# One condition in a list scheduler's port model: small two-input VectorE operations and GpSimd

## The chip, the cores and the metric

The kernel runs on one core of a Trainium2 chip. The metric is the device time of one execution in microseconds, the median of several runs. A profiled execution has a time of its own, which is given beside the length of its trace, the span.

## The reference: what is computed

The input x has 2048 tokens of 512 elements. It is normalised per token, and the result is the sum of x, a linear attention block on the normalised tokens and a dense block on the same.

```python
xn = _layernorm(x)                       # 2048 x 512, eps 1e-5
q, k, v = split(xn @ wqkv)               # 32 heads of 16
phi = lambda t: where(t > 0, t + 1, exp(t)) + 1e-6
kv = sum over tokens of phi(k) v^T       # per head
z  = sum over tokens of phi(k)
o  = (phi(q) kv) / (phi(q) z + 1e-6)
A  = o @ wo
B  = relu(xn @ w1 + b1)**2 @ w2 + b2     # 1376 hidden
out = x + A + B
```

Everything is float32. The kernel splits each operand of a product into a high and a low part in a faster TensorE format and adds three products, so each logical matmul is three of 128x512.

## The kernel before, in words

The token axis is cut into 16 tiles of 128 (NT), grouped in 4 blocks of 512 (NB, TB = 4).

**First part: keys.** For each tile i the kernel takes mean and variance on VectorE (measure: bn_stats, bn_aggr), the root on ScalarE (roots: Ln, then Exp), three small VectorE operations that refine it and the scaling itself (normalise). The scaled tile xp[i] is turned, by TensorE for the first 8 tiles (turned_pe) and by DMAs with a VectorE transpose for the others, and split in high and low (transposed: tiles xs0h, xs0l, xs1h, xs1l). TensorE then forms the key projection (project, tiles pk in PSUM), ScalarE and VectorE apply phi and split the result (phi_k, parts: tiles k and pk), ScalarE and GpSimd split the scaled tile itself (tokens: tile tok, the only large work of GpSimd), and TensorE accumulates xp^T phi(k) over all tiles (kx).

**Second part.** The queries, the attention's output and the dense block are done for two pairs of blocks with one level of Strassen's scheme: weights and their sums are split into operands (ops) that go out to DRAM (wd) and come back, the tokens' sums (T) likewise stay on chip, hidden values (rr, rf, c) are squared or divided, split on ScalarE and VectorE (parts_of: tiles s), and multiplied into PSUM (second).

**The order of the work is planned, not written.** The function body doesn't issue instructions. `nc` is a Program whose engines are Recorders; each call becomes a Task with its predecessors (add), and a duration from a formula (cost). emit then asks order for a sequence and issues it. order plays the list up to 150 times (ROUNDS):

- play is a list scheduler with one lane per engine. TensorE's tasks, and all tasks recorded ahead of `nc.fixed = len(nc.tasks)` (set after kx(0)), keep their recorded order on their engine. Behind that, each of VectorE, ScalarE, GpSimd and SyncE picks, among the tasks that are ready within 0.1 us, the one with the earliest due time.
- press looks at every wait of TensorE over 0.1 us in that play, follows the chain of causes back and moves the due times of the tasks on it earlier.
- The play with the earliest end gives the order that is issued.

Two engines meet in the model at one more point. A task with `lock` set starts no earlier than the end of the last locked task, and holds the lock for its own length:

```python
            if t.lock:
                t.start = max(t.start, locked)
                locked = t.start + t.dur
```

GpSimd's tensor_tensor has the lock (in this kernel the low halves of tok, and one of wkl). VectorE's tensor_tensor and scalar_tensor_tensor have it when no input is in PSUM and, before the change, when the output has more than 64 elements per partition. In cost, n is that number of output elements, and src the largest count of any operand. VectorE's two-input operations are modelled at 0.157 us + src/960.

The operations with two inputs in SBUF and 64 elements or fewer are the three refining ones of normalise, on 1 to 3 elements (one per tile of the group):

```python
        nc.vector.scalar_tensor_tensor(u, var, 1e-5, y0, op0=OP.add, op1=OP.mult)
        nc.vector.scalar_tensor_tensor(u, u, -0.5, y0, op0=OP.mult, op1=OP.mult)
        nc.vector.scalar_tensor_tensor(r, u, 1.5, y0, op0=OP.add, op1=OP.mult)
```

They write tile y. The groups of tiles are (0), (1), (2), (3), (4, 8, 9), (5, 10), (6, 11), (7, 12), (13, 14) and (15); normalise of the first four is recorded ahead of nc.fixed, of the others behind it. Since every instruction is issued from emit, nearly all lines of the profile carry its line, L301, and groups are told apart by their tiles.

Of the kernel before, what the change touches and what calls it, by code (L numbers as in the profile page):

```python
# [74 lines left out]
class Program:  # L75
# [59 lines left out]
    def cost(self, t, out, ins):  # L135
        n = 1
        for s, k in list(out.ap)[1:]:
            n *= k
        src = n
        for a in ins:  # L140
            m = 1
            for _, k in list(a.ap)[1:]:
                m *= k
            src = max(src, m)
        t.lock, t.size, t.lag = False, 0, 0.06
        if t.engine == "tensor":
            wide = t.name == "matmul" and ins[0].dtype != F32
            t.dur, t.lag = (0.0135 + n / 2400 if wide else 0.055 + n / 2400 if t.name == "transpose" else 0.11 + n / 1200), 0.23
        elif t.engine == "scalar" and t.name != "dma_start":
            ps = any(map(in_psum, ins))  # L150
            t.dur = (0.2 if ps else 0.22) + src / 1250 + (0.09 if t.kw.get("bias") is not None and n > 64 and not isinstance(t.kw.get("bias"), float) else 0)
        elif t.engine == "vector":
            a, b = self.DVE.get(t.name, (0.1, 0.5))
            t.dur = a + src * b / 960
            t.lock = t.name in ("tensor_tensor", "scalar_tensor_tensor") and n > 64 and not any(map(in_psum, ins))
        elif t.engine == "gpsimd" and t.name != "dma_start":
            t.dur = 0.2 + src * 2.3 / 1000 if t.name == "tensor_tensor" else 0.3
            t.lock = t.name == "tensor_tensor"
        else:
            b = 1  # L160
            for s, k in out.ap:
                b *= k
            run = 1
            for a in (out, *ins):
                d = list(a.ap)
                c = d[-1][1] if d[-1][0] == 1 else 1
                run = min(run, c) if run > 1 else c
            t.size, t.lag = 4 * b, 2.8 if b > P * P else 2.0
            t.dur = 0.43 if out.ap[0][1] == P and run >= 512 else 0.62 if ins and isinstance(ins[0], View) and isinstance(out, View) else 0.5 if t.engine != "gpsimd" else 1.2
            t.size = t.size * max(1.0, (0.009 + run * 4 / 27e3) / (run * 4 / 24e3)) if run > 1 else b * 150  # L170
# [1453 lines left out]
```

## Time and profile before

| what | value |
|---|---|
| time, median of 3 runs | 409.05 us (408.73 to 409.63) |
| time of the profiled execution | 408.82 us |
| its span | 407.1 us |
| TensorE busy | 399.6 us in 1793 matmuls and transposes |
| VectorE busy | 353.2 us in 600 instructions |
| ScalarE busy | 269.4 us in 461 instructions |
| GpSimd busy | 28.0 us in 50 instructions |
| DMA | 95.68 MB, mean 235 GB/s |
| granted TensorE clock | 0.999 |

PE is TensorE, PEld its weight loads, DVE VectorE, ACT ScalarE, POOL GpSimd, SP SyncE. A row of a group gives its engine and operation, output<-inputs by tile name (buffer numbers left out), shapes, count, then busy time, mean duration in ns, and the idle time of the engine just before, with what ended it. A row of the chain or of the order of time begins with start and length in us. A row by stage gives the stage, its length, and the busy time and count of each engine.

### The profile page before, as it was taken

What the parts mean: (1) busy time and instruction counts of PE and PEld (TensorE: products, weight loads), DVE (VectorE), ACT (ScalarE), POOL (GpSimd) and SP (SyncE); (2) the same over time, 40 slices, a digit from 0 to 9 for tenths busy, and PEclk for the clock granted to TensorE, in tenths of its full rate; (3) what the DMA queues carried; (4) which work ended last, traced back from release to release, by engine and by line L of the source; (5) the groups of instructions that cost most, each with busy time, mean ns of one, the idle gap of its engine ahead of it and who ended that gap; (6) DMA issues with size and microseconds to landing.
All of it is one profiled execution on the core that took longest, in us unless ns stands there. A gap on an engine that the chain in (4) does not pass through costs nothing.

```text
span 407.1 us, 5594 instructions
## 1 busy us (share of the span) xinstructions
PE 399.6 (98%) x1793; PEld 330.4 (81%) x1793; DVE 353.2 (87%) x600; ACT 269.4 (66%) x461; POOL 28.0 (7%) x50
## 2 busy tenths in 40 slices
PE   8999999999999999999999999999999999999994
PEld 7787888788888888888888888888888888888883
DVE  5899898799878898999889989899989989786784
ACT  5785665675858897889886343366888777545440
POOL 2232322220000000000000000000000000000001
PEclk9999999999999999999999999999999999999999
DMA  7871455933997679667359998999767789979424
GB/s 230 292 194 43 104 155 125 280 100 151 327 323 287 233 280 306 248 241 260 155 194 361 258 339 275 370 298 330 280 223 271 263 219 258 256 277 281 157 54 103
DMA packets 78674, 95.68 MB, mean 235 GB/s; under 512 B 39186, under 2 KB 50450, under 8 KB 78388
## 3 DMA queue, kind: packets, MB, share of 16 engines
q1 hardware_dynamic: 76404, 94.53, 73.4%
q10 hardware_dynamic: 2144, 0.52, 0.6%
q0 software_dynamic: 96, 0.26, 0.3%
q8 instruction: 14, 0.23, 0.2%
q14 instruction: 16, 0.13, 0.1%
HBM read 57.81 MB, written 35.39 MB: 229 GB/s over the span
## 4 chain that ended last, share of the span: by engine, by line
PE 95%; DVE 2%; DMA 1%; ACT 1%; issue 0%
PE ps L301 52%; PE acc L301 42%; DMA x<-in_A_x_dram 1%; DVE y L301 1%; DVE xp L301 0%; DVE res L301 0%; DVE o L301 0%; DVE st L301 0%; ACT k L301 0%; DVE pk L301 0%; DVE xs0l L301 0%; ACT t L301 0%; ACT xs0h L301 0%; DVE mv L301 0%
## 5 line engine op out<-in xcount | busy, mean ns | idle before, releaser
L301 PE MATMUL ps<-s,ops 128*128 128x512 f32 x405 | 94.9, 389 | 0.0
L301 PEld LDWEIGHTS ps<-s,ops 128*128 128x128 f32 x405 | 76.0, 188 | 15.8
L301 PE MATMUL acc<-s,ops 128*128 128x512 f32 (+1 forms) x270 | 62.2, 382 | 0.0
L301 PEld LDWEIGHTS acc<-s,ops 128*128 128x128 f32 x270 | 49.6, 188 | 9.9
L301 ACT ACTIVATE s<-rr 128x512 fp32r<-128x512 f32 x54 | 33.8, 631 | 20.9 <-DVE s L301 12.0
L301 PE MATMUL acc<-pk,tok 128*128 128x512 f32 x192 | 47.2, 394 | 0.0
L301 DVE TENSOR_TENSOR s<-rr,s 128x512 fp32r<-128x512 f32 x54 | 36.8, 688 | 11.8 <-ACT s L301 10.6
L301 PEld LDWEIGHTS acc<-pk,tok 128*128 128x128 f32 x192 | 35.4, 188 | 8.3 <-DVE pk L301 0.6
L301 PE MATMUL ps<-T,ops 128*128 128x512 f32 x168 | 41.4, 390 | 0.0
L301 PE MATMUL acc<-T,ops 128*128 128x512 f32 x168 | 41.2, 389 | 0.0
L301 PEld LDWEIGHTS acc<-T,ops 128*128 128x128 f32 x168 | 31.5, 188 | 6.6
L301 PEld LDWEIGHTS ps<-T,ops 128*128 128x128 f32 x168 | 31.5, 188 | 6.5
L301 POOL TENSOR_TENSOR tok<-xp,tok 128x512 fp32r<-128x512 f32 x16 | 21.5, 1347 | 43.8 <-ACT tok L301 43.8
L301 PE MATMUL ps<-xs0h,ops 128*128 128x512 f32 x72 | 23.7, 389 | 0.0
L301 ACT ACTIVATE rr<-acc 128x512 f32<-128x512 f32 x23 | 13.6, 589 | 11.5 <-PE acc L301 11.1
L301 DVE TENSOR_TENSOR ops<-raw,ops 128x512 fp32r<-128x512 f32 (+1 forms) x28 | 18.7, 676 | 1.6 <-ACT ops L301 1.6
L301 ACT ACTIVATE ops<-raw 128x512 fp32r<-128x512 f32 (+1 forms) x28 | 15.8, 576 | 5.2 <-PE acc L301 1.8
L301 PE MATMUL acc<-xs0h,ops 128*128 128x512 f32 x56 | 18.4, 389 | 0.0
L301 DVE TENSOR_TENSOR rr<-acc,rr 128x512 f32<-128x512 f32 x21 | 14.4, 687 | 2.9 <-PE acc L301 1.6
L301 POOL DMA_DIRECT2D out_dram<-res x2 | 1.5, 729 | 215.5 <-DVE res L301 213.0
L301 ACT ACTIVATE k<-ps 128x512 f32<-128x512 f32 x16 | 9.5, 593 | 10.1 <-PE ps L301 9.9
L301 PEld LDWEIGHTS ps<-xs0h,ops 128*128 128x128 f32 x72 | 13.5, 188 | 2.8
(158 smaller groups left out, 772.1 us busy)
## 6 DMA issues: line engine op xcount, KB each, us to landing
wd<-ops SPq DMA_DIRECT2D x35, 512.0 KB, 4.8
ops<-wd SPq DMA_DIRECT2D x31, 512.0 KB, 5.5
ops<-wd SPq DMA_DIRECT2D x56, 256.0 KB, 4.1
wd<-made SPq DMA_DIRECT2D x10, 512.0 KB, 5.9
res<-in_A_x_dram SPq DMA_DIRECT2D x32, 128.0 KB, 5.6
wd<-ops SPq DMA_DIRECT2D x13, 256.0 KB, 3.7
out_dram<-res SPq DMA_DIRECT2D x24, 128.0 KB, 4.7
x<-in_A_x_dram SPq DMA_DIRECT2D x5, 512.0 KB, 5.9
```

The source lines that it names most:

```text
L301: getattr(getattr(self.nc, t.engine), t.name)(*map(real, t.args), **{k: real(a) for k, a in t.kw.items()})
```

## The change

One line of cost loses one condition, so that VectorE's tensor_tensor and scalar_tensor_tensor have the lock at any size when no input is in PSUM. Durations, predecessors, first due times and the recorded list of tasks stay; so do all instructions and their operands. What can differ is the order in which VectorE, ScalarE, GpSimd and SyncE issue theirs.

```diff
         elif t.engine == "vector":
             a, b = self.DVE.get(t.name, (0.1, 0.5))
             t.dur = a + src * b / 960
-            t.lock = t.name in ("tensor_tensor", "scalar_tensor_tensor") and n > 64 and not any(map(in_psum, ins))
+            t.lock = t.name in ("tensor_tensor", "scalar_tensor_tensor") and not any(map(in_psum, ins))
```

## The prediction

> **What bounds the kernel now.** I read the page from the top: span, busy time by engine, granted clock by slices.
>
> ```profile
> span 407.1 us, 5594 instructions
> PE 399.6 (98%) x1793; PEld 330.4 (81%) x1793; DVE 353.2 (87%) x600; ACT 269.4 (66%) x461; POOL 28.0 (7%) x50
> PEclk9999999999999999999999999999999999999999
> ```
>
> TensorE is busy for 98% of the span at the full granted clock, and VectorE for 87%. The two lie that close, so the question is where TensorE ever waits. The table by stage tells it:
>
> ```profile
> 23.30:48.00 24.70, 24.24 (x114) 19.58 (x113) 23.56 (x52) 16.70 (x36) 7.21 (x10) 1.00 0.37 92
> 48.00:90.00 42.00, 41.99 (x186) 34.46 (x185) 36.49 (x55) 27.06 (x50) 11.69 (x17) 1.00 0.62 166
> 90.00:150.00 60.00, 60.00 (x283) 50.24 (x282) 52.14 (x88) 45.65 (x77) 0.00 (x0) 1.00 0.76 267
> 150.00:250.00 100.00, 100.00 (x443) 82.81 (x442) 91.75 (x149) 71.59 (x118) 0.52 (x1) 1.00 0.79 262
> 250.00:350.00 100.00, 100.00 (x443) 82.77 (x442) 91.88 (x155) 69.67 (x115) 0.00 (x0) 1.00 0.89 273
> 350.00:399.00 49.00, 49.00 (x218) 40.58 (x217) 36.65 (x56) 22.65 (x37) 0.80 (x1) 1.00 0.66 199
> ```
>
> After the length of a stage come the busy times of TensorE, its weight loads, VectorE, ScalarE and GpSimd. Between 48 and 399 us TensorE is busy for 350.99 of 351 us. In 23.3 to 48 it idles for 0.46 us, and there VectorE is busy for 23.56 of 24.70 us (95%): this is the stage in which VectorE is the one that is late. What is left of the span is the start and the tail after the last matmul.
>
> The list of TensorE's own waits names the place, and the chain that ended last shows the same stretch in order of time:
>
> ```profile
> PE ps L301 <- DVE xp L301: 0.5, 1, 0.5
> ```
>
> ```profile
> 17.14 2.89 PE acc L301 x12
> ...
> 20.47 3.01 PE acc L301 x12
> ...
> 30.40 1.18 DVE y L301
> ...
> 33.25 2.76 PE acc L301 x12
> 36.01 3.30 PE ps L301 x16
> 39.30 2.77 PE acc L301 x12
> 42.07 3.16 PE ps L301 x16
> 45.23 2.77 PE acc L301 x12
> 48.01 2.72 PE ps L301 x12
> ...
> 77.93 3.01 PE acc L301 x12
> 80.94 2.72 PE ps L301 x12
> ```
>
> Twelve matmuls take 2.72 us when nothing holds them (the rows at 48.01 and 80.94). From the excess of the other rows I count what TensorE loses to late operands: 0.17 + 0.29 at 17 and 20 us, 0.46 before the row at 33.25, 0.04 + 0.05 + 0.05 in the rows of 2.76 and 2.77, 0.14 in 3.30 against 3.16, and 0.29 at 77.93. That is **1.5 us in the whole kernel**, the most that a better order of the same work can win between start and tail.
>
> **The change part by part.** No instruction is added, removed or resized. The lock flag of the planner's VectorE two-input tasks loses its condition n > 64. The only tasks with two on-chip inputs and at most 64 elements are the three scalar_tensor_tensor of each normalise (tile y, 1 to 3 elements): ten groups, 30 tasks. Four groups lie ahead of nc.fixed, where every engine keeps its recorded order, and six behind it, 18 tasks. In the planner's play these 18 now start only when GpSimd's last tensor_tensor is done. Do they wait on the chip? The rows of groups and of time say yes:
>
> ```profile
> L301 POOL TENSOR_TENSOR tok<-xp,tok 128x512 fp32r<-128x512 f32 x16 | 21.5, 1347 | 43.8 <-ACT tok L301 43.8
> L301 DVE SCALAR_TENSOR_TENSOR y<-mv,y 128x2 f32<-128x2 f32 x4 | 3.6, 908 | 0.1
> L301 DVE SCALAR_TENSOR_TENSOR y<-mv,y 128x1 f32<-128x1 f32 x5 | 0.7, 147 | 0.0
> ```
>
> ```profile
> 30.02 1.53 POOL L301 TENSOR_TENSOR tok<-xp,tok 128x512 fp32r<-128x512 f32 x1 [3.21 <-ACT tok L301]
> ...
> 30.32 1.25 DVE L301 SCALAR_TENSOR_TENSOR y<-mv,y 128x2 f32<-128x2 f32 x1
> ...
> 31.99 1.92 DVE L301 TENSOR_SCALAR xp<-x,mv,y 128x512 f32<-128x512 f32 x4
> ...
> 32.59 0.65 PE L301 MATMUL ps<-ident,xp 128*128 128x128 f32 x4 [0.46 <-DVE xp L301]
> ```
>
> A two-element operation has a mean of 908 ns where its one-element sister has 147, and the one at 30.32 ends at 31.57, 0.02 us after GpSimd's at 31.55. The Trainium skill, SBUF — State Buffer, section "Who interferes with whom", says that a VectorE instruction with two SBUF inputs contends with a GpSimd instruction that reads SBUF; the trace agrees, down to two elements. By that rule alone the new model is the truer one and the sum would be the gain below without the loss.
>
> **The gain.** Four two-element operations cost 4 x (0.908 - 0.147) = 3.0 us of VectorE time that the present plan doesn't know of. They are on the end's path only where TensorE waits: behind the operation at 30.32 stand the other two y operations, the scaling to xp and then TensorE's transposes, which start 0.46 us late. With the 0.14 of the row at 36.01 I put the aimed gain at **0.6 us**. Its bounds are 0 (the planner finds no better place in a stage where VectorE is 95% busy) and 1.5 us (all excess goes).
>
> **The loss.** The plan is the best of 150 rounds of a greedy play; each round moves due times by the waits of the round before, and an operation is chosen among those ready within 0.1 us. A start that shifts by 1 us at 30 us changes these choices all the way down. So VectorE, ScalarE, GpSimd and SyncE get another order between 23 and 399 us, not only around y, while TensorE keeps its own. Behind 48 us the present order loses 0.3 us. The new one can't win there, and it has these margins:
>
> ```profile
> L301 ACT ACTIVATE s<-rr 128x512 fp32r<-128x512 f32 x54 | 33.8, 631 | 20.9 <-DVE s L301 12.0
> L301 DVE TENSOR_TENSOR s<-rr,s 128x512 fp32r<-128x512 f32 x54 | 36.8, 688 | 11.8 <-ACT s L301 10.6
> DVE s L301 <- ACT s L301: 15.6, 27, 1.0
> ```
>
> VectorE has 8.2 us free in each 100 us of the two long stages, and much of its idling is already the second half of a split waiting for ScalarE's first half (27 times, 15.6 us). Where another order lets a split slip by one place, TensorE waits for one VectorE operation (0.69) or the pair (0.63 + 0.69 = 1.32 us). What a new order costs is not in the trace. From below it is 0 (the model's orders hold on the chip as this one does); from above I take four whole splits, 4 x 1.32 = 5.3 us. The nearest row is a slip of one VectorE operation, 0.69 us, and I take three in 351 us: **2.1 us**. That "three" is a choice, not a reading; the only firm support is that the present count is nearly zero and can only rise.
>
> Queues: the DMAs of xTd, wd and ops are SyncE tasks and move with the plan too. The queues gain nothing to issue, so I cost that at nothing; the cover is the DMA engines' share, 0.62 to 0.89 in the stages behind 48 us. If it is gone, a late ops tile costs up to the 5.5 us from issue to landing, which I leave outside the sum:
>
> ```profile
> ops<-wd SPq DMA_DIRECT2D x31, 512.0 KB, 5.5
> ```
>
> Sum against the profiled execution: 408.82 (span 407.1 and 1.7 around it) - 0.6 + 2.1 = 410.3. The median of the runs lies 0.23 above that execution, so **410.5 us**.
>
> **Rivals.**
> *Only the gain.* The search is good enough to leave TensorE unbroken behind 48 us again. For it: the modelled costs are plainly close (the present order holds for 351 us), and the change mends a wait that was modelled as nothing. Time: 409.05 - 0.6 = 408.45, and with all excess gone 407.55; as a case I centre it on 408.1. It decides from the point at which the row at 33.25 starts without the 0.46 and no new wait stands behind 48 us. Chance 0.32.
>
> *The wait changes its owner.* The planner puts the y operations ahead of GpSimd's tok, and the next VectorE operation of the group, the scaling to xp, meets it instead, unmodelled before and after:
>
> ```profile
> 55.34 1.34 POOL L301 TENSOR_TENSOR tok<-xp,tok 128x512 fp32r<-128x512 f32 x1 [3.74 <-ACT tok L301]
> 55.44 1.52 DVE L301 TENSOR_SCALAR xp<-x,mv,y 128x512 f32<-128x512 f32 x1
> L301 DVE TENSOR_SCALAR xp<-x,mv,y 128x512 f32<-128x512 f32 x16 | 9.2, 600 | 0.3
> ```
>
> The scaling at 55.44 takes 1.52 against a mean of 0.60, some 0.9 us of waiting. Paid once in place of the 1.1 of the y at 30.32, it gives 409.05 - 0.2 = 408.9. The Trainium skill (SBUF — State Buffer, the same section) lists tensor_scalar among the operations that can take the shared ports; the row above agrees, and by that rule the change mends half of the group. Chance 0.2, together with an order that hardly changes or whose gain and loss cancel, within 0.3 us of 409.05.
>
> *The change does nothing* would need that no y met a lock in the model; the four groups of two elements stand so near to tok that I count it in the chance above.
>
> **How the numbers follow.** Forecast (slower, 410.5) 0.48, only the gain 0.32, owner or cancelling 0.2. The forecast's own range is 409.7 to 413.7 (one slip without the gain, 0.69, to four whole splits less the gain: 409.05 + 5.3 - 0.6). The range of all takes in the other cases: low 407.5 (all excess gone), high 413.5. About 0.2% (0.8 us) is what a measurement of this kernel can tell from no change, since three runs span 408.73 to 409.63. Of the 0.32, 0.24 lies beyond that, the rest is the same; of the forecast 0.45 lies beyond. So faster 0.24, same 0.31 (0.2 + 0.08 + 0.03), slower 0.45.
>
> **What would show it.** The gain: two-element y operations at 0.15 to 0.2 us, TensorE without idle time in 23 to 48 us, VectorE's busy time in that stage down by up to 3 us. The loss: pieces of the chain behind 48 us longer than 2.72 per twelve matmuls, and ACT or VectorE s, ops, rr or T as releaser of TensorE in the list of waits. The owner's rival: xp operations over 1 us in greater number. The forecast is wrong if TensorE's busy time between 48 and 399 is whole again, or if the loss sits in the start or the tail, which I hold still: the last store ends on the same chain of transposes and adds whatever the plan.

## The result, and the profile after

| | before | after |
|---|---|---|
| median of the runs (the three of before above are among its six) | 409.35 us (408.73 to 410.06, 6 runs) | 407.72 us (407.62 to 408.01, 6 runs) |
| profiled execution, its span | 408.82, 407.1 us | 408.01, 406.3 us |

The ratio is 0.9961, 95% interval 0.9948 to 0.9974: **faster by 0.4%**, 1.6 us, where slower by 0.35% (410.5 us) was forecast. The time lies below the forecast's own range, 409.7 to 413.7, and inside the range of all cases, 407.5 to 413.5. The sign is the other one.

The table by stage of the changed kernel, and TensorE's list of waits:

```profile
23.30:48.00 24.70, 24.70 (x118) 20.42 (x117) 22.46 (x53) 17.48 (x38) 7.44 (x12) 1.00 0.46 114
48.00:90.00 42.00, 42.00 (x187) 34.79 (x186) 36.61 (x56) 26.15 (x47) 12.56 (x15) 1.00 0.58 168
90.00:150.00 60.00, 60.00 (x282) 50.24 (x282) 49.59 (x83) 46.87 (x79) 0.00 (x0) 1.00 0.75 259
150.00:250.00 100.00, 100.00 (x443) 82.81 (x442) 92.50 (x150) 70.20 (x115) 0.52 (x1) 1.00 0.81 251
250.00:350.00 100.00, 100.00 (x443) 82.75 (x442) 91.64 (x155) 71.38 (x116) 0.00 (x0) 1.00 0.94 289
350.00:399.00 49.00, 49.00 (x221) 40.66 (x220) 38.78 (x60) 22.18 (x36) 0.79 (x1) 1.00 0.66 193
```

```profile
PE ps L301 <- DVE odds L301: 1.1, 1, 1.1
PE acc L301 <- DVE y L301: 0.3, 1, 0.3
```

Between 23.3 and 48 us TensorE idled 0.46 us before; now 24.70 of 24.70 us are busy. Behind 48 us it is unbroken again. The two waits left stand in the first 8 us. The chain of the changed kernel:

```profile
20.68 2.99 PE acc L301 x12
23.67 3.17 PE ps L301 x16
26.84 2.75 PE acc L301 x12
29.60 3.16 PE ps L301 x16
32.76 2.77 PE acc L301 x12
35.53 3.16 PE ps L301 x16
38.69 2.75 PE acc L301 x12
...
77.30 2.72 PE acc L301 x12
80.02 2.72 PE ps L301 x12
```

From the row at 20.68 to that at 32.76 are 12.08 us; before it was 33.25 - 20.47 = 12.78. The y, xp and ACT steps that stood in this chain before are gone from it, and at 77.30 a plain 2.72 stands in place of 3.01. The rows of 2.99 and of 2.75 to 2.77 are nearly as long as before. The y operations themselves, by group and in order of time:

```profile
L301 DVE SCALAR_TENSOR_TENSOR y<-mv,y 128x2 f32<-128x2 f32 x4 | 0.6, 161 | 0.7 <-ACT y L301 0.7
L301 DVE SCALAR_TENSOR_TENSOR y<-y 128x1 f32<-128x1 f32 x10 | 3.1, 305 | 0.3
```

```profile
28.42 0.16 DVE L301 SCALAR_TENSOR_TENSOR y<-mv,y 128x2 f32<-128x2 f32 x1 [0.45 <-ACT y L301]
28.61 0.36 DVE L301 SCALAR_TENSOR_TENSOR y<-y 128x2 f32<-128x2 f32 x2
29.01 0.55 DVE L301 TENSOR_SCALAR xp<-x,mv,y 128x512 f32<-128x512 f32 x1
```

The group that ran at 30.3 us, just behind GpSimd's tok, now runs at 28.4, ahead of it, and the mean of the two-element operation falls from 908 to 161 ns. Two one-element ones behind 46 us wait now (1.02 us at 47.12, 0.76 at 54.17; the mean of the ten goes from 176 to 305 ns), where TensorE isn't held by them.

**A ledger.** TensorE does the same matmuls in the same order in every kernel of this study, so its time can be compared piece by piece. The columns, called periods below, run from the first weight load of kx for tile 2 to that for tile 3, from 3 to 4, 4 to 5, 10 to 13, and from there to the last weight load of the program, in us of the profiled execution. Tiles 5 to 10 are left out: they take the same time in every kernel but e2.

| kernel | 2-3 | 3-4 | 4-5 | 10-13 | 13-end |
|---|---|---|---|---|---|
| before | 6.60 | 6.05 | 5.93 | 16.61 | 312.49 |
| before, second profile (e4) | 6.61 | 6.05 | 5.93 | 17.28 | 312.45 |
| after | 5.92 | 5.93 | 5.91 | 16.32 | 312.50 |

Against the least seen (5.92, 5.92, 5.91, 16.32) the order before loses 0.7 + 0.1 us at tiles 2 to 4 in each profile, and 0.29 in one and 0.96 in the other at tiles 10 to 13. The changed kernel loses nothing. The sum, 1.1 to 1.8 us, has the measured 1.6 within it. The start of the program, up to the first of these loads of tile 0, is recorded ahead of nc.fixed and has the same order in all of them; it differs from execution to execution (16.6 to 17.1 us in these three), which is why the spans of the two first profiles differ by 0.8 only. The last column is the one to keep in mind: **312.5 us in all three**.

### The profile page after: what moved, and what is told of

Read it like the earlier page. It is cut to its first block, busy times and chain, and to the rows that moved or that the text cites. A ratio compares the mean times of both kernels' runs of the same rounds, so it can differ in the third digit from the quotient of the medians.

```text
span 406.3 us, 5591 instructions
## 1 busy us (share of the span) xinstructions
PE 399.2 (98%) x1793; PEld 330.8 (81%) x1793; DVE 351.6 (87%) x600; ACT 270.2 (66%) x461; POOL 28.9 (7%) x50
## 4 chain that ended last, share of the span: by engine, by line
PE 96%; DVE 1%; DMA 1%; issue 0%
PE ps L301 53%; PE acc L301 43%; DMA x<-in_A_x_dram 1%; DVE res L301 0%; DVE o L301 0%; DVE st L301 0%; DVE xp L301 0%; DVE y L301 0%; DVE mv L301 0%
## 5 line engine op out<-in xcount | busy, mean ns | idle before, releaser
L301 PE MATMUL ps<-s,ops 128*128 128x512 f32 x405 | 94.9, 389 | 0.0
L301 PEld LDWEIGHTS ps<-s,ops 128*128 128x128 f32 x405 | 76.0, 188 | 15.8
L301 PE MATMUL acc<-s,ops 128*128 128x512 f32 (+1 forms) x270 | 62.2, 382 | 0.0
L301 PEld LDWEIGHTS acc<-s,ops 128*128 128x128 f32 x270 | 49.6, 188 | 9.9
L301 ACT ACTIVATE s<-rr 128x512 fp32r<-128x512 f32 x54 | 33.8, 631 | 21.0 <-DVE s L301 11.0
L301 PE MATMUL acc<-pk,tok 128*128 128x512 f32 x192 | 47.1, 394 | 0.0
L301 DVE TENSOR_TENSOR s<-rr,s 128x512 fp32r<-128x512 f32 x54 | 36.5, 688 | 8.8 <-ACT s L301 7.4
L301 PEld LDWEIGHTS acc<-pk,tok 128*128 128x128 f32 x192 | 35.4, 188 | 7.9 <-DVE pk L301 0.6
L301 PE MATMUL ps<-T,ops 128*128 128x512 f32 x168 | 41.4, 390 | 0.0
L301 PE MATMUL acc<-T,ops 128*128 128x512 f32 x168 | 41.2, 389 | 0.0
L301 PEld LDWEIGHTS acc<-T,ops 128*128 128x128 f32 x168 | 31.5, 188 | 6.6
L301 PEld LDWEIGHTS ps<-T,ops 128*128 128x128 f32 x168 | 31.5, 188 | 6.5
L301 POOL TENSOR_TENSOR tok<-xp,tok 128x512 fp32r<-128x512 f32 x16 | 22.5, 1408 | 41.5 <-ACT tok L301 25.6
L301 PE MATMUL ps<-xs0h,ops 128*128 128x512 f32 x72 | 23.6, 389 | 0.0
L301 ACT ACTIVATE ops<-raw 128x512 fp32r<-128x512 f32 (+1 forms) x28 | 15.9, 574 | 4.7 <-PE ps L301 2.2
L301 PE MATMUL acc<-xs0h,ops 128*128 128x512 f32 x56 | 18.4, 389 | 0.0
L301 DVE TENSOR_TENSOR ops<-raw,ops 128x512 fp32r<-128x512 f32 (+1 forms) x28 | 16.5, 599 | 1.7 <-ACT ops L301 1.7
L301 DVE TENSOR_TENSOR rr<-acc,rr 128x512 f32<-128x512 f32 x21 | 14.4, 688 | 4.0 <-PE acc L301 2.8
L301 ACT ACTIVATE rr<-acc 128x512 f32<-128x512 f32 x23 | 13.5, 588 | 6.2 <-PE acc L301 6.1
L301 ACT ACTIVATE k<-ps 128x512 f32<-128x512 f32 x16 | 9.5, 595 | 11.8 <-PE ps L301 11.6
L301 POOL DMA_DIRECT2D out_dram<-res x2 | 1.5, 726 | 215.5 <-DVE res L301 213.0
L301 PEld LDWEIGHTS ps<-xs0h,ops 128*128 128x128 f32 x72 | 13.5, 188 | 2.8
```

The costliest lines, as they stand in the source:

```text
L301: getattr(getattr(self.nc, t.engine), t.name)(*map(real, t.args), **{k: real(a) for k, a in t.kw.items()})
```

## The experiments

Theory A: the gain is made where the y operations stand, because the plan now sees their wait, so that orders made without it are worse. Its rival, theory B: the order is a fresh draw and the gain is luck. Beside these, C and D on what varies at 78 us. All kernels are compared with the kernel before on the same chip; its medians there were 409.05 to 409.53 us. Where an experiment adds lines ahead of emit, its rows have L302 to L314 in place of L301.

**Which part of the order holds the gain: e1 and e2.** The planner runs twice, with the old and the new flag, and the two orders are spliced: tasks that both plans start before 50 us go in one order, the rest in the other.

```diff
+            self.order()            # once per flag; starts[0] old, starts[1] new
+        first = {t for t in self.tasks if all(s[t] < 50 for s in starts)}
+        early, late = starts[1], starts[0]          # e2: starts[0], starts[1]
+        key = lambda t: (0, early[t], t.index) if t in first else (1, late[t], t.index)
```

> Order spliced: what both plans start before 50 us comes in the changed kernel's order, all the rest in the order of before. Theory A (the gain is made in the stage of the y operations, because the plan sees their wait): TensorE without idle time from 23 to 48 us, two-element y operations near 0.16 us, time 408.2 to 408.7, at least 0.6 below before. Theory B (the gain is a lucky redraw of the later part, unrelated to y): within 0.3 us of before, near 409.3.

> The other splice: what both plans start before 50 us in the order of before, the rest in the changed kernel's order. Theory A: TensorE's late transposes at 32.6 us are still there, time 408.9 to 409.4. Theory B: 407.7 to 408.3, with nearly all of the gain.

Measured: e1 407.67 us, 0.9964 (0.9952 to 0.9977), the whole gain and more than either theory gave it; e2 409.57 us, 1.0010 (1.0001 to 1.0019), none, and 0.2 above the range of theory A. In e1 the periods are 5.93, 5.92, 5.93, 16.32 with 312.46 behind: the early order alone clears the loss at 78 us too, though that part runs in the order of before. In e2 the periods 6.61 and 6.04 of before are back. It also has a new wait of its own, 1.1 us of TensorE for pk, which neither whole plan has. It comes with the seam between the two plans, at tiles 7 to 8 (6.83 us in place of 5.44). So e2 tells less of the late order than e1 does of the early one:

```profile
PE acc L314 <- DVE pk L314: 1.1, 1, 1.1
PE ps L314 <- DVE xp L314: 0.5, 1, 0.5
```

**Is it the second input that makes y wait: e3.** The order of before; each small operation is issued as one-input operations with the second operand as a scalar per partition.

```diff
+            if t.engine == "vector" and t.name == "scalar_tensor_tensor" and t.dur < 0.2:
+                o, i, c, y0 = map(real, t.args)
+                for k in range(o.shape[1]):
+                    self.nc.vector.tensor_scalar(o[:, k:k + 1], i[:, k:k + 1], c, y0[:, k:k + 1], **t.kw)
+                continue
```

> Order of before, but each small two-input y operation is issued as one tensor_scalar per token tile, with the second operand as a scalar per partition (the same values; 43 instructions in place of 30). If the wait of y comes from the second tensor input: y operations under 0.2 us each with tok running beside them, VectorE's busy time in 23 to 48 us down by some 2 us, TensorE's wait of 0.46 us gone, time 408.4 to 408.9. If any small VectorE operation waits for GpSimd: y operations up to 1.3 us again, time 409.3 or above.

Measured: 407.89 us, 0.9969 (0.9956 to 0.9981), more than expected. (There are 48 such instructions, not the 43 of the expectation.) At the place where y waited, in order of time:

```profile
30.08 1.52 POOL L306 TENSOR_TENSOR tok<-xp,tok 128x512 fp32r<-128x512 f32 x1 [3.21 <-ACT tok L306]
30.38 0.33 DVE L304 TENSOR_SCALAR y<-mv,y 128x1 f32<-128x1 f32 x2
30.62 0.58 DVE L304 TENSOR_SCALAR y<-y 128x1 f32<-128x1 f32 x4
31.12 2.14 DVE L306 TENSOR_SCALAR xp<-x,mv,y 128x512 f32<-128x512 f32 x4
```

Six operations run beside tok in 0.8 us, where the first one alone took 1.25. The periods are 5.91 and 5.91. The Trainium skill, SBUF — State Buffer, section "Who interferes with whom", says that a VectorE instruction with at most one SBUF input, outside the two-port modes, does not contend with GpSimd; these rows agree, for operations on one element. So with the order before unchanged, taking the wait from y gives 0.3%: the wait is the cause of the early loss. In the profiled execution, the slowest of its five (408.35), 0.63 us at tiles 10 to 13 is still lost.

**What varies at 78 us: e4, e5, e9, e13.** e4 is the kernel before once more. e5 issues the first two wv operations directly ahead of the third, e9 ScalarE's split of raw_z behind the split of raw, e13 both; otherwise the order of before.

```diff
+        for t in ts:                                # e9, e13
+            if t.engine == "scalar" and t.name == "activation" and isinstance(t.args[1], View) and t.args[1].place.name == "raw_z_0":
+                t.start += 5.6
+        wv = [t for t in ts if t.engine == "vector" and "out" in t.kw and t.kw["out"].place.name == "wv"]
+        for k, t in enumerate(wv[:2]):              # e5, e13
+            t.start = wv[2].start - 0.002 + 0.001 * k
```

> The kernel before, once more, for a second profile: its six runs spread over 1.3 us, the changed kernel's over 0.4. Theory C: the spread is in the order of before at 75 to 80 us, where VectorE stands waiting for the load of raw_v (2.4 us) and TensorE loses 0.29; another profile then shows another loss there (0 to 1 us), the rest the same within 0.1. Otherwise the difference sits in the first 8 us, the loads of x, and is no matter of the order. Time 409.35 within 0.3.

> Order of before with one thing moved: the first two of VectorE's four wv operations, on which it stands for 2.4 us until raw_v lands, are issued directly ahead of the third. Theory C (the second part of the gain is that raw_v lands earlier against TensorE): the loss of 0.3 to 0.7 us at 78 us goes, 408.4 to 408.9, and the runs spread over less than 0.6; TensorE's 0.46 us at 32.6 and the long y operations stay. If that wait is covered: 409.2 with the spread of before, 1.3.

> Order of before with one thing moved: ScalarE's split of raw_z, for whose load it stands 1.07 us at 24.5, goes six operations back, behind the split of raw, into a gap of 1.4 us. Theory D (the spread of before and a part of its loss come from that landing, which passes through k, y and xp into TensorE): runs within 0.6 us of each other, median 408.2 to 408.8. If the landing isn't on TensorE's path in the other executions: 409.3 and a spread of 1 us or more.

> Order of before with both moves, of ScalarE's raw_z split and of VectorE's first two wv operations. TensorE's loss at 78 us should go, the 0.7 us of the y operation in the period that starts at 30 us stay: 408.4 to 408.7, spread below 0.7. If it stays at 409.2, more than the profiles show is lost to y itself.

Measured: e4 409.20 us. Its second profile has a row of 0.7 us among TensorE's waits that the first lacks, and this chain around it:

```profile
PE acc L301 <- ACT pk L301: 0.7, 1, 0.7
```

```profile
76.93 0.61 DVE k L301
...
77.57 0.64 ACT pk L301
...
78.34 2.99 PE acc L301 x12
```

So theory C's place was right: the part of the loss that varies sits there. Its cause, VectorE's wait for raw_v, was not enough. e5 measured 409.18 us, 0.9994 (0.9985 to 1.0003); e9 409.33, 1.0004 (0.9995 to 1.0013); e13 409.11, 0.9997 (0.9988 to 1.0006): no gain from any of the moves, and runs that spread over 0.7 to 1.1 us, each more than its theory allowed. Theory D falls too: e9 takes 6.61 at 2-3, as before, and 17.24 at 10-13. In e5's profile the loss at 78 us is gone (16.33), but that is the fastest of its eleven executions (408.64); in e13's it is back (17.01), so that e13's time tells nothing more of y. The chain of e13 shows a second way to the same loss; it has the queue of SyncE, a landing and ScalarE in it:

```profile
65.97 0.59 SPq L301
...
66.61 1.97 DMA xg<-xp
...
71.00 6.08 DMA raw<-in_A_wqkv_dram
...
77.42 0.62 ACT pk L301
...
78.18 3.00 PE acc L301 x12
```

ScalarE stands waiting for raw, and its pk goes out behind that, just as VectorE stood waiting for raw_v. Both loads are issued by SyncE behind a burst of 16 transfers xg<-xp that begins when the last tokens are scaled. SyncE's rows of before and of e1:

```profile
58.53 10.07 SPq L301 DMA_DIRECT2D xg<-xp  x16
68.70 0.53 SPq L301 DMA_DIRECT2D wd<-ops  x1
69.35 0.37 SPq L301 DMA_DIRECT2D raw_v<-in_A_wqkv_dram  x1
```

```profile
56.98 10.08 SPq L314 DMA_DIRECT2D xg<-xp  x16
67.16 0.53 SPq L314 DMA_DIRECT2D wd<-ops  x1
67.81 0.37 SPq L314 DMA_DIRECT2D raw_v<-in_A_wqkv_dram  x1
```

With the early order changed, the burst begins 1.55 us earlier, raw_v follows 1.54 us earlier (TensorE's row at 48.01 only 0.86, at 47.15), and the loss at 78 us goes in the same late order. The rows show burst and load moving together. That the waits of y make the last scalings late, and so the burst and TensorE's loss, is argued; no run moved the burst by itself. A late burst is not enough by itself: e10 below has it at 58.69 us, and raw issued at 69.57 (69.83 before), and yet no loss. The order of ScalarE differs there. First the rows of before, then those of e10:

```profile
76.66 0.42 ACT L301 ACTIVATE ops<-raw 128x256 fp32r<-128x256 f32 x1 [0.15 <-DMA raw<-in_A_wqkv_dram]
77.16 0.63 ACT L301 ACTIVATE pk<-k 128x512 fp32r<-128x512 f32 x1
```

```profile
73.93 0.63 ACT L302 ACTIVATE pk<-k 128x512 fp32r<-128x512 f32 x1 [0.23 <-DVE k L302]
75.23 0.92 ACT L302 ACTIVATE ops<-raw 128x512 fp32r<-128x512 f32 x2
```

Before, the pk that TensorE needs is issued behind the split that waits for raw; in e10 it goes ahead of it. So the loss seems to need both, a late load and an operation that TensorE needs behind it. No run moved that pk by itself either, so the cause of this part stays open.

**Is it the truer model or a luckier order: e6 to e8, e10 to e12.** The first due times are shifted by 0 to 0.06 us in a fixed pattern, so that the search ends in another order, with the old flag (e6, e7, e10, e11: K = 4, 5, 1, 2) and with the new one (e8, e12: K = 2, 1).

```diff
             t.due = min(t.due, when)
+            t.due += 0.01 * (t.index * K % 7)
```

> The flag as before, but all first due times shifted by 0 to 0.06 us in a fixed pattern, so that the search ends in another order. Theory A (orders made without the wait meet it on the chip): two-element y operations near 0.9 us on average again, TensorE idle somewhere between 23 and 62 us, 408.7 to 410.5. Theory B (the order is luck): as likely 407.5 as 409.2.

> The flag as before, a second pattern of shifts. Theory A: above 408.4, with a y or xp operation over 0.9 us ahead of a late TensorE. Theory B: as likely 407.5 as 409.2.

> The changed flag, first due times shifted in a pattern as in the two redraws of the old one. Theory A: two-element y operations mostly below 0.3 us, TensorE without idle time from 23 to 48 us, 407.4 to 408.3. Theory B: anywhere from 407.5 to 410.

> The flag as before, a third pattern of shifts of the first due times. Theory A (orders made without the small operations' wait are worse): 408.7 or above. Theory B (before's order was an unlucky one, either flag gives such or better): 407.8 to 408.5, as the first two redraws.

> The flag as before, a fourth pattern. Theory A: 408.7 or above. Theory B: 407.8 to 408.5.

> The changed flag, a second pattern. Theory A: 407.4 to 408.3 and below every redraw of the old flag. Theory B: 407.7 to 409, mixed with those of the old flag.

| kernel | flag | us | ratio to before | 2-3 | 3-4 | 4-5 | 10-13 | 13-end |
|---|---|---|---|---|---|---|---|---|
| e6 | old | 408.02 | 0.9967 (0.9955 to 0.9980) | 5.93 | 6.10 | 5.92 | 16.32 | 312.55 |
| e7 | old | 408.31 | 0.9974 (0.9965 to 0.9983) | 5.92 | 6.35 | 5.92 | 16.32 | 312.66 |
| e10 | old | 407.81 | 0.9962 (0.9949 to 0.9974) | 5.93 | 5.91 | 5.93 | 16.32 | 312.45 |
| e11 | old | 408.14 | 0.9975 (0.9965 to 0.9985) | 5.94 | 5.91 | 5.93 | 16.34 | 312.48 |
| after | new | 407.72 | 0.9961 (0.9948 to 0.9974) | 5.92 | 5.93 | 5.91 | 16.32 | 312.50 |
| e8 | new | 408.16 | 0.9970 (0.9959 to 0.9981) | 5.94 | 6.31 | 5.91 | 16.32 | 312.45 |
| e12 | new | 408.75 | 0.9984 (0.9973 to 0.9994) | 5.93 | 6.58 | 6.32 | 16.32 | 312.50 |

Theory A said that orders made with the old flag are slow. All four are faster than before, by 0.25 to 0.38%, where the three with the new flag are by 0.16 to 0.39%. **It falls in this form**: the change is faster because it replaced an unlucky order, in which the wait of y fell on TensorE's path, and each of the six redraws was faster too, with either flag. The old flag's orders do meet the wait, as theory A said (two-element y operations of 648 ns on average in e6, 354 in e7), but TensorE loses only 0 to 0.4 us in the early periods. The slowest of the new flag, e12, has another owner of the wait:

```profile
35.27 1.29 POOL L302 TENSOR_TENSOR tok<-xp,tok 128x512 fp32r<-128x512 f32 x1 [2.55 <-ACT tok L302]
35.29 1.56 DVE L302 TENSOR_SCALAR xp<-x,mv,y 128x512 f32<-128x512 f32 x1
```

The three y operations are ahead of tok now, and the scaling behind them starts 0.02 us too late and waits until tok ends at 36.56. TensorE loses 0.66 us in that period.

**The scaling locked too: e14 to e16.** The new flag, and tensor_scalar among the operations that have the lock; first due times as they are (e14) and with the two patterns of e12 and e8 (e15: K = 1, e16: K = 2).

```diff
-            t.lock = t.name in ("tensor_tensor", "scalar_tensor_tensor") and not any(map(in_psum, ins))
+            t.lock = t.name in ("tensor_tensor", "scalar_tensor_tensor", "tensor_scalar") and not any(map(in_psum, ins))
```

> The changed flag, and the lock for tensor_scalar with no PSUM input too (the scaling to xp). Owner theory (a plan that knows only y's wait puts the wait on xp): no xp over 0.6 us on the chain into TensorE's transposes, 407.5 to 408.0. If the flag and its extension don't matter: 407.7 to 408.8, as the redraws with either flag.

> The same, with the pattern of shifts that gave 408.75 with the changed flag alone, where an xp operation of 1.56 us stands behind tok at 35.3 us. Owner theory: 407.5 to 408.1. Otherwise 407.7 to 408.8.

> The same, with the pattern that gave 408.16 with the changed flag alone. Owner theory: 407.5 to 408.1. Otherwise 407.7 to 408.8.

Measured: 407.62 us, 0.9968 (0.9955 to 0.9980); 407.64, 0.9965 (0.9953 to 0.9978); 408.00, 0.9976 (0.9967 to 0.9984). All three lie in the owner theory's ranges, but e16's 408.00 lies in its rival's too, and the other two are less than 0.1 us below it. With the pattern of e12 the time falls by 1.1 us, 0.8 by the ratios; the periods 3-4 and 4-5, 6.58 and 6.32 in e12, are 5.91 and 5.93. In e14 an xp of 1.55 us still stands behind tok at 40.53, but TensorE doesn't wait for it.

The runs were on several chips, so kinds of orders are compared by their ratios to before on the same chip. The means are 0.9970 with both locked (three orders), 0.9972 with the changed flag (three) and 0.9970 with the old flag redrawn (four). The time doesn't tell the three models apart. The ledger speaks for the fullest, weakly: in the periods shown its three orders lose nothing, those of the changed flag 0, 0.4 and 1.1 us, the old flag's redraws 0, 0, 0.2 and 0.4. With so few orders that isn't shown. e14 and the changed kernel (407.62 and 407.72) can't be told apart.

## Why the prediction was wrong

- **What bounds the kernel: right.** TensorE, with what it loses in 23 to 48 us and at 78 us. All that the ledger shows as won lies there.
- **The wait of y: right.** The two-element operations went from 908 to 161 ns, and TensorE's 0.46 us are gone. e3 shows the wait by itself.
- **The gain, 0.6 us: too small.** The aimed place gave 0.7 + 0.1. The 0.29 at 77.93 was counted only in the bound of 1.5, and behind 48 us the new order was said to have nothing to win. Two things were missed: that this loss depends on the early order too (e1 clears it with the late order untouched), and that one profile shows one execution. It was 0.96 in another. The queues, put at nothing, may have a part in it: in e1 raw_v is issued 1.54 us earlier. That the profiled 408.82 was near the fastest of its runs stood in the table of times. The 1.5 itself was read too high: 0.6 of it is the excess in rows of 2.89, 2.99 to 3.01 and 2.75 to 2.77 ahead of 48 us, and these rows are nearly as long in the changed kernel. That its bound, 407.55, comes so close to the measured time is partly luck.
- **The loss, 2.1 us: the step that failed.** The forecast took three slips of a VectorE operation behind 48 us because "the present count is nearly zero and can only rise". Measured, in all eighteen profiles, ten of them of orders searched anew (the changed kernel's among them), the stretch from tile 13 to the end takes 312.44 to 312.66 us, and in those ten the one from tile 10 to 13 takes 16.32 to 16.34. The price of another order there is 0 to 0.2 us in place of 2.1; only the seam of e2 cost more. What the forecast read as a lucky order that a new draw would spoil was the planner's ability, as ten draws without a loss there show: 351 us without a gap over some 500 VectorE operations is not one draw but many placements that all held. The margins quoted beside it (8.2 us of idle VectorE in 100) fit that too.
- **The draw mattered in the other direction.** The forecast asked what a redraw could spoil late, and not whether the order before was a poor draw early. What new orders do lose, they lose early: 0.2 to 0.4 us in e6, e7 and e8, 1.1 in e12. The row by which to ask it was there: a stage with VectorE at 95%, a wait that the plan didn't know, and TensorE late just behind it.
- **The rivals.** "Only the gain" came true at its lower end (407.55 to 408.45 were its bounds), with the part at 78 us that it hadn't aimed at. "The wait changes its owner" isn't what this order did, but e12 did just that, at 0.66 us in one period.

## What to carry to other kernels

When a list scheduler's order changes, look first at what it may lose where the present order already loses. Here the stretch that the planner had filled without a gap was filled again in ten orders of ten, and the losses moved about in the stage where VectorE is 95% busy. A single change of a planner should be judged against a few redraws with the old model, or a lucky order will be taken for a better model. When a wait for something that two engines share is mended for one operation, look at the next in line, which can meet the same holder, as xp did in e12.

## What the runs showed of the hardware

- A VectorE operation on one or two elements with two SBUF inputs waits for the whole rest of a GpSimd tensor_tensor: 1.25 us in place of 0.16 on two elements (before), 1.02 on one (after, at 47.12). A tensor_scalar on a single element, with its second operand as a scalar per partition, doesn't (six in 0.8 us beside tok in e3), while a tensor_scalar on 512 elements does (1.56 in e12 in place of 0.55).
- SyncE issues the 16 xg transfers in 10.1 us, 0.63 each, and issues what stands behind them in its order only then: raw_v follows 10.8 us behind the start of the burst both before (58.53 to 69.35) and in e1 (56.98 to 67.81).
